# The second token chunk's attention spread over one more step of the first chunk's feed-forward loop, with a tile per block, and two weight decodings moved from steps 3 and 6 to steps 5 and 8

## The chip, the cores and the metric

The kernel runs on one core of a Trainium2 chip. The metric is the device time of one execution in microseconds (us); the time before is a median of 3 runs. Five engines with a queue each work side by side: PE (matrix products), DVE (vector work), ACT (activations and copies), POOL, and SP, which issues the transfers. Each engine executes its own queue strictly in the order in which it stands.

## What the kernel computes

```python
# windowed attention: 4 x 8 heads, 576 tokens, head size 64, each token sees the 64 up to itself
x = attn(q, k, v)                        # then heads are merged: 2304 x 512
# a dense feed-forward layer
h = x @ w_in                             # 512 -> 2048
g = where(h >= 1, h, where(h <= -1, 0, (h + 1) ** 2 / 4))
x = g @ w_out                            # 2048 -> 512
# a mixture of 8 experts, one per token
e = argmax(x @ w_gate + modality_bias[modality_id])
out = gate_w * (relu(x @ w1[e]) @ w2[e])
```

The dense weights `w_in` and `w_out` arrive as 64-bit floats and are decoded to 32 bits on the core.

## The kernel before

The 2304 tokens form 6 chunks of 384 (NC = 6); a chunk has 6 attention blocks of 64 tokens (BPC = 6), so that blocks 0 to 5 belong to chunk 0 and 6 to 11 to chunk 1. The work is software-pipelined: while chunk c goes through the feed-forward layer, the attention of chunk c+1 is done between its steps. The change touches only chunk 0's feed-forward loop, `step0(f)`, f = 0 to 15, one step for each slice of 128 hidden units. Within it the order on PE, DVE, ACT and POOL is the order in which the code is written (a manual schedule); SP's order is manual throughout.

What a step f of that loop issues, as far as the change and the prediction speak of it:

- `act2(0, f-1)` (L517, DVE): the nonlinearity of the step before, which also frees the PSUM tile `h` of that step. Tile `g` up to step 8, tile `u` after.
- `dec_clamp`, `dec_merge` (L279 to L292, DVE): eight instructions for each *pair* of weight slices that is decoded in this step. `turn[f]` lists the pairs: one for each step and a second one in the steps that `TWICE` names. `dec_abs` (L272, ACT) is the pair's first part, issued a step earlier; `dec_load` (L266, SP) fetches a pair three pairs later, once the buffer is merged.
- For the blocks of chunk 1, one new block in each of the steps 1 to 6 (`FIRST`): `att_mm` (L370, PE, scores into an `aux` PSUM tile), `att_max` (L385, DVE) and `att_exp` (L395, ACT) in the step in which a block begins; `att_norm` (L407, L408 on DVE, L416 on ACT) a step later; `att_tr` (L425, transposes on PE, copied by ACT, L430) two steps later; `att_pv` (L447, PE) and `att_x` three steps later. `att_x` copies the result into chunk 1's input, high part by ACT (`xh`, L467), low part by DVE (`xl`, L468). The `aux` tag has three PSUM buffers, used in turn by scores, transposes and results.
- `l1(0, f)` (L476, later L497, PE), `relu` (L503, L504, ACT), and `l2(0, f-2)` (L543, later L549, PE). From step FS = 9 on, the products are made of a high and a low part of each operand: `split_x0` makes them of chunk 0's input (`x0h` on ACT L349, `x0l` on DVE L350), `split_hi` and `split_lo` (L312 on ACT, L317 on DVE) of the weights.
- From step FJ = 10 on, a step also does chunk 1's first layer, `l1(1, f)`, which reads `xh` and `xl` of all six blocks 6 to 11.

Of the kernel before, what the change touches and what calls it, by code (L numbers as in the profile page):

```python
# [17 lines left out]
P = 128  # L18
# [3 lines left out]
KD = DM // P  # L22
FF = 2048
NF = FF // P
# [8 lines left out]
BPC = CT // BLK  # L33
# [38 lines left out]
def moe_kernel(ctx, tc, qT, kT, v, w_in, w_out, mod, wg, wgT, mbias, w1, w2, cst, tri, empty, out, spec):  # L72
    nc = tc.nc
    V, A, G, T, SP = nc.vector, nc.scalar, nc.gpsimd, nc.tensor, nc.sync
# [15 lines left out]
    def tile_of(shape, name, dt=F32, tag=None, bufs=1):  # L90
        pool = sb if (tag or name) in WIDE else sm
        return pool.tile(shape, dt, name=name, tag=tag or name, bufs=bufs)

    def aux(shape, name):
        return ps.tile(shape, F32, name=name, tag="aux", bufs=3)

    WB = KD * P
# [8 lines left out]
    def lend(f, lo, n=WB):  # L106
        if f not in lent:
            lent[f] = tile_of([P, 2 * WB], f"lent{f}", tag=f"T{NF + f}")
        return lent[f][:, lo * WB : lo * WB + n]
# [27 lines left out]
    def window(i):  # L137
        return (P, (i - 1) * BLK) if i % SPB else (BLK, i * BLK)

    def load_v(i):  # L140
        n, w0 = window(i) if i else (P, 0)
        if i == 1:
            vs[i] = vs[0]
            return
        vs[i] = lend(2 + i // 2, i % 2) if i < BPC else tile_of([P, DM], f"v{i}", tag="v", bufs=2)
        SP.dma_start(vs[i][:n], v[w0 : w0 + n, :])
# [57 lines left out]
    PRE = 3  # L204
    LAG = 2
    FS, FJ = 9, 10
    TWICE = (3, 6)

    def part(kind, f, lo):
        return parts[kind, f][0][:, lo * WB : (lo + 1) * WB]  # L210
# [1 line left out]
    def raw_home(p, u):  # L212
        if pairs[p][u] == lone_kf:
            return tile_of([P, WB], "lone", I32)
        if p not in raws:
            raws[p] = tile_of([P, 2 * WB], f"raw{p}", I32, tag=f"T{p}")
        return raws[p][:, u * WB : (u + 1) * WB]
# [22 lines left out]
    turn, p = [], 1  # L240
    for f in range(NF + 1):
        turn.append(list(range(p, min(p + 1 + (f in TWICE), NPR))))
        p += len(turn[-1])
# [14 lines left out]
    def words(p, u):  # L258
        w = raw(p, u).rearrange("p (n w) -> p n w", w=2)
        return w[:, :, 0], w[:, :, 1]  # L260
# [22 lines left out]
    def dec_merge(p, us=(0, 1)):  # L283
        if p < NPR:
            t = dts[p]
            for u in us:
                V.scalar_tensor_tensor(
                    t[u], words(p, u)[1], -0x40000000, t[u], op0=ALU.bitwise_and, op1=ALU.bitwise_or
                )
            for u in us:  # L290
                w = raw_home(p, u)
                V.scalar_tensor_tensor(  # L292
                    w, words(p, u)[0], 29, t[u], op0=ALU.logical_shift_right, op1=ALU.bitwise_or
                )
                whole[pairs[p][u]] = w.bitcast(F32)
# [46 lines left out]
    def split_x0(j):  # L342
        if not j:
            hi = [tile_of([P, 2 * WB], f"x0h{n}", F32R, tag=f"T{NF + 10 + n}") for n in range(2)]
            hi = [t[:, : KH * CT].rearrange("p (k n) -> p k n", k=KH) for t in hi]
            xs[0] = (hi, tile_of([P, KD, CT], "x0l", F32R, tag="xl", bufs=2))
        hi, lo = xs[0]
        ks = slice(j * KH, (j + 1) * KH)
        A.copy(hi[j], whole_x[0][:, ks])  # L349
        V.tensor_tensor(lo[:, ks], whole_x[0][:, ks], hi[j].bitcast(F32), op=ALU.subtract)  # L350

    at, xos = {}, {}
    PAIRED = 2 * BPC

    def att_sc(i):
        att_mm(i)
        att_max(i)
# [17 lines left out]
    def att_max(i):  # L375
        sc = scs.pop(i)
        n = window(i)[0]
        if i < BPC:
            s = lend(8 + i, 0).rearrange("p (k n) -> p k n", k=KD)
        else:  # L380
            s = tile_of([P, KD, P], f"s{i}", tag="s", bufs=2)
        mask = C["m1"] if i % SPB else C["m0"]
        mx = tile_of([P, KD], f"mx{i}", tag="mx", bufs=4)
        for hp in range(KD):
            V.tensor_tensor_reduce(  # L385
                s[:, hp, :n], sc[:, hp, :n], mask, -0.125, 3.0e38, ALU.add, ALU.min, mx[:, hp : hp + 1]
            )
        at[i] = (s, mx)
# [31 lines left out]
    def att_tr(i):  # L420
        s, _ = at[i]
        n = window(i)[0]
        pt = aux([P, KD, P], f"pt{i}")
        for hp in range(KD):
            T.transpose(pt[:n, hp, :], s[:, hp, :n], C["ident"])  # L425
        if i < BPC:
            ts = lend(8 + i, 1).rearrange("p (k n) -> p k n", k=KD)
        else:
            ts = tile_of([P, KD, P], f"ts{i}", tag="ts", bufs=2)
        (V.tensor_copy if i < BPC - 2 else A.copy)(ts[:n], pt[:n])  # L430
        at[i] = ts

    def att_pv(i):
        o = 0
        if i < BPC:
            xo = ps.tile([P, KD, BLK], F32, name=f"xo{i}", tag="h", bufs=2)
        elif i < PAIRED:
            xo = aux([P, KD, BLK], f"xo{i}")
        else:
            o = i % GB  # L440
            xo = xos[i - 1] if o else aux([P, KD, GT], f"xo{i}")
        ts = at.pop(i)
        vt = vs.pop(i)
        w = window(i)[0]
        for hp in range(KD):
            for a in range(2):
                T.matmul(  # L447
                    xo[a * D : (a + 1) * D, hp, o * BLK : (o + 1) * BLK],
                    vt[:w, (2 * hp + a) * D : (2 * hp + a + 1) * D],
                    ts[:w, hp, a * BLK : (a + 1) * BLK],  # L450
                    start=True,
                    stop=True,
                )
        xos[i] = xo

    def att_x(i):
        xo = xos.pop(i)
        c, n = divmod(i, BPC)
        dst = slice(n * BLK, (n + 1) * BLK)
        if i >= PAIRED:  # L460
            xos.pop(i + 1)
            dst = slice(n * BLK, n * BLK + GT)
        if c == 0:
            A.copy(whole_x[0][:, :, dst], xo)
            return
        xh, xl = xs[c]
        A.copy(xh[:, :, dst], xo)  # L467
        V.tensor_tensor(xl[:, :, dst], xo, xh[:, :, dst].bitcast(F32), op=ALU.subtract)  # L468
# [63 lines left out]
    def gsplit_lo(c, f, u):  # L532
        gh, gl = gs[c, f]
        V.tensor_tensor(gl, u, gh.bitcast(F32), op=ALU.subtract)  # L534
# [466 lines left out]
    def att_loads(i):  # L1001
        if i % GB == 0 and i + GB < NB:
            load_k(i // GB + 1)
        if i >= PAIRED:
            load_v(i)
# [42 lines left out]
    def step0(f):  # L1048
        split0 = f - 1 >= FS
        join = f >= FJ  # L1050
        at_step = {f - st: BPC + k for k, st in enumerate(FIRST)}
        if f == NF - 3:
            free.extend(f"T{NF + k}" for k in (14, 15))
        if f >= 1:
            act2(0, f - 1)
            if split0:
                gsplit_hi(0, f - 1, us[0, f - 1])
        if f - 1 >= FJ:
            act2(1, f - 1)
        for kf in soon.get(f, []):  # L1060
            split_lo()
        if split0:
            gsplit_lo(0, f - 1, us[0, f - 1])
        for p in turn[f]:
            dec_clamp(p)
            dec_merge(p)
        if 3 in at_step:
            att_pv(at_step[3])
            att_x(at_step[3])
        if 2 in at_step:  # L1070
            att_tr(at_step[2])
        if 1 in at_step:
            load_v(at_step[1])
        if 0 in at_step:
            att_mm(at_step[0])
            att_loads(at_step[0])
        for p in turn[f]:
            dec_load(p + 3)
        l1(0, f)
        relu(0, f)  # L1080
        for p in turn[f + 1][:1]:
            dec_abs(p)
        if 1 in at_step:
            att_norm(at_step[1])
        if 0 in at_step:
            att_max(at_step[0])
            att_exp(at_step[0])
        if f in (FS - 2, FS - 1):
            split_x0(f - FS + 2)
        if join:  # L1090
            l1(1, f)
            relu(1, f)
        if f >= LAG:
            l2(0, f - LAG)
        for p in turn[f + 1][1:]:
            dec_abs(p)
        for kf in soon.get(f + 1, []):
            split_hi(kf)
        if f == FS - 1:
            token_bias()  # L1100
        if f == NF - 1:
            free.extend(f"T{NF + k}" for k in (10, 11))
            hold_back(gs[0, f - 1][0].bitcast(F32))
            wgb.append(tile_of([P, E, DM], "wgb", tag="dec"))
            SP.dma_start(
                wgb[0].rearrange("p e d -> p (e d)"),
                wgT.rearrange("(o e) d -> o (e d)", o=1).broadcast_to([P, E * DM]),
            )
# [7 lines left out]
    for n in range(len(its) + LAG):  # L1116
        c, f = its[n] if n < len(its) else (NC, n - len(its))
# [151 lines left out]
```

## Time and profile before

| what | value |
| --- | --- |
| time, median of 3 runs (lowest, highest) | 736.42 us (736.12, 738.23) |
| the profiled execution: its own time, its span in the trace | 735.82 us, 734.2 us |
| PE busy | 717.1 us, 98% of the span |
| PE weight loads (PEld) busy | 625.5 us, 85% |
| DVE busy | 474.2 us, 65% |
| ACT busy | 390.1 us, 53% |
| POOL busy | 127.0 us, 17% |

Times in the rows below are counted from the start of the span. A busy time counts an engine's own instructions; the share is an average over stages that differ, and the stage that the change touches lies between 25 and 95 us of the span.

### The profile page before, as it was taken

Reading aid. Unit: us, or ns where it says so; the run is one execution under the profiler, and the core shown is the slowest. Engines: PE = TensorE matmul, PEld = TensorE weight load, DVE = VectorE, ACT = ScalarE, POOL = GpSimd, SP = SyncE. Lnnn points to the kernel's source line nnn. Section 1 sums busy time; section 2 is a strip of 40 time slices with the busy share of each in tenths; the row PEclk is TensorE's granted clock in tenths of the full one; section 3 lists DMA queues with packets and bytes.
Section 4 is the critical chain, followed back from the end, with each engine's and each line's share of the span. In section 5 each row is a group of like instructions: output and inputs, shape, how many; then the busy total and the mean of one; then the engine's idle time right before and its main releaser. Section 6 shows DMA issues by size and latency. Waiting matters only on the chain. (4 is left out here: it accounts for less than half of the span.)

```text
span 734.2 us, 12536 instructions
## 1 busy us (share of the span) xinstructions
PE 717.1 (98%) x4217; PEld 625.5 (85%) x4217; DVE 474.2 (65%) x1439; ACT 390.1 (53%) x942; POOL 127.0 (17%) x185
## 2 busy tenths in 40 slices
PE   8899999999999999999999999999999999999994
PEld 6555689888998989888989898999989989898984
DVE  5999897797397528852696638866775545453600
ACT  6777778666545535554555445645444544453511
POOL 3200000113001201120111502031058322201010
PEclk9999999999999999999999999999999999999998
DMA  9997413322121203220310015245455754444310
GB/s 327 334 346 258 147 55 127 118 66 80 52 86 59 80 15 108 73 80 16 108 59 29 2 41 171 67 93 191 158 137 171 232 181 155 159 159 160 115 43 7
DMA packets 48570, 89.26 MB, mean 122 GB/s; under 512 B 6976, under 2 KB 16320, under 8 KB 48368
## 3 DMA queue, kind: packets, MB, share of 16 engines
q1 hardware_dynamic: 44064, 78.36, 32.3%
q0 software_dynamic: 4288, 9.79, 4.6%
q8 instruction: 35, 0.57, 0.3%
q14 instruction: 39, 0.32, 0.1%
q10 hardware_dynamic: 144, 0.22, 0.1%
HBM read 78.89 MB, written 9.87 MB: 121 GB/s over the span
## 5 line engine op out<-in xcount | busy, mean ns | idle before, releaser
L497 PE MATMUL h<-xh,w 128*128 128x384 f32 x640 | 179.4, 341 | 0.0
L549 PE MATMUL py<-w,gh 128*128 128x512 f32 x522 | 162.1, 393 | 0.0
L497 PEld LDWEIGHTS h<-xh,w 128*128 128x128 f32 x640 | 117.1, 188 | 2.3
L549 PEld LDWEIGHTS py<-w,gh 128*128 128x128 f32 x522 | 96.6, 188 | 16.2
L497 PE MATMUL h<-xl,w 128*128 128x384 f32 x320 | 107.4, 336 | 0.0
L796 DVE TENSOR_TENSOR e<-wr,e 128x512 fp32r<-128x512 f32 x112 | 74.7, 690 | 45.2 <-ACT e L795 43.2
L549 PE MATMUL py<-w,gl 128*128 128x512 f32 x261 | 102.7, 396 | 0.0
L858 PE MATMUL hp<-zh,e 128*128 128x384 f32 x384 | 100.9, 336 | 0.0
L503 ACT ACTIVATE u<-h,half 128x384 f32<-128x384 f32 x96 | 55.5, 578 | 82.3 <-PE h L497 70.8
L873 PE MATMUL yo<-e,hm 128*128 128x512 f32 x348 | 99.0, 394 | 0.0
L517 DVE SCALAR_TENSOR_TENSOR u<-u,h 128x384 f32<-128x384 f32 x81 | 44.7, 552 | 68.3 <-ACT u L504 67.8
L603 DVE CUSTOM_DVE_ANT_0 prod<-y,wgb 128x512 f32<-128x512 f32 x120 | 85.3, 710 | 1.3
L529 ACT CAST gh<-u 128x384 fp32r<-128x384 f32 x81 | 41.6, 514 | 67.5 <-DVE u L517 29.1
L795 ACT CAST e<-wr 128x512 fp32r<-128x512 f32 x112 | 66.0, 616 | 18.4 <-DMA wr<-in_w 18.2
L873 PEld LDWEIGHTS yo<-e,hm 128*128 128x128 f32 x348 | 64.2, 188 | 12.4
L858 PEld LDWEIGHTS hp<-zh,e 128*128 128x128 f32 x384 | 69.6, 188 | 0.8
L418 POOL TENSOR_TENSOR s<-s,sm 128x512 f32<-128x512 f32 (+1 forms) x24 | 26.2, 1093 | 222.4 <-DVE sm L408 158.1
L858 PE MATMUL hp<-zl,e 128*128 128x384 f32 x192 | 64.3, 335 | 0.0
L534 DVE TENSOR_TENSOR gl<-u,gh 128x384 fp32r<-128x384 f32 x81 | 45.5, 562 | 26.7 <-ACT gh L529 25.7
L497 PEld LDWEIGHTS h<-xl,w 128*128 128x128 f32 x320 | 60.2, 188 | 1.9
L549 PEld LDWEIGHTS py<-w,gl 128*128 128x128 f32 x261 | 48.9, 188 | 10.4
L395 ACT ACTIVATE s<-s,mx 128x128 f32<-128x128 f32 (+1 forms) x120 | 45.9, 385 | 11.7 <-DVE mx L385 11.7
(218 smaller groups left out, 1049.5 us busy)
## 6 DMA issues: line engine op xcount, KB each, us to landing
wr<-in_w SPq DMA_DIRECT2D x112, 256.0 KB, 2.9
q<-in_qT SPq DMA_DIRECT2D x32, 256.0 KB, 3.4
dec<-in_w_in SPq DMA_DIRECT2D x16, 512.0 KB, 5.5
dec<-in_w_out SPq DMA_DIRECT2D x16, 512.0 KB, 4.3
v<-in_v SPq DMA_DIRECT2D x27, 256.0 KB, 3.0
k<-in_kT SPq DMA_DIRECT2D x15, 384.0 KB, 4.7
yd<-y SPq DMA_DIRECT2D x18, 256.0 KB, 2.2
wgb<-in_wgT SPq DMA_DIRECT2D x1, 2048.0 KB, 6.9
```

What stands on the lines that cost most here:

```text
L395: A.activation(s[:, hp, :n], s[:, hp, :n], AF.Exp, bias=mx[:, hp : hp + 1], scale=-1.0, accum_out=sm[:, hp : hp + 1],)
L497: T.matmul(h, wi(f, a)[:, k, :], b, start=n == 0, stop=n == 3 * KD - 1)
L503: A.activation(u, h, AF.Relu, bias=half, scale=0.5)
L517: V.scalar_tensor_tensor(g, u, 1.0, h, op0=ALU.min, op1=ALU.max)
L529: A.copy(gh, u)
L534: V.tensor_tensor(gl, u, gh.bitcast(F32), op=ALU.subtract)
L549: T.matmul(ys[c][t], a[:, sl], wo(f, b), start=f == first and n == 0, stop=f == last and n == 2)
L603: V.tensor_tensor_reduce(prod, yt[t], wgb[0][:, e, :], 1.0, 0.0, ALU.mult, ALU.add, lg[:, t, e : e + 1])
L795: A.copy(wpart(i, p, 0), t)
L796: V.tensor_tensor(wpart(i, p, 1), t, wpart(i, p, 0).bitcast(F32), op=ALU.subtract)
L858: T.matmul(hp, w1s(i, f, k, a), b[:, k, :], start=n == 0, stop=n == 3 * KD - 1)
L873: T.matmul(yo, a[f][:, sl], w2s(i, f, b), start=n == 0, stop=n == 3 * NF2 - 1)
```

## The change

Chunk 1's transposes move from two steps after the scores to three, its products with the values and the copies from three to four, and the loads of the values from one to two. Scores and their transposed copies get a tile for each block (`own`, on tags T18 to T23, which chunk 0's attention has used before) instead of two rotating buffers each. `TWICE` becomes steps 5 and 8, and `split_x0` moves from steps 7 and 8 to steps 6 and 7.

```diff
-    TWICE = (3, 6)
+    TWICE = (5, 8)
...
+    own = {}
...
+        elif i < PAIRED:
+            own[i] = tile_of([P, 2, WB], f"st{i}", tag=f"T{NF + 2 + i - BPC}")
+            s = own[i][:, 0].rearrange("p (k n) -> p k n", k=KD)
         else:
             s = tile_of([P, KD, P], f"s{i}", tag="s", bufs=2)
...
+        elif i < PAIRED:
+            ts = own.pop(i)[:, 1].rearrange("p (k n) -> p k n", k=KD)
         else:
             ts = tile_of([P, KD, P], f"ts{i}", tag="ts", bufs=2)
...
+        if 4 in at_step:
+            att_pv(at_step[4])
+            att_x(at_step[4])
         if 3 in at_step:
-            att_pv(at_step[3])
-            att_x(at_step[3])
+            att_tr(at_step[3])
         if 2 in at_step:
-            att_tr(at_step[2])
-        if 1 in at_step:
-            load_v(at_step[1])
+            load_v(at_step[2])
...
-        if f in (FS - 2, FS - 1):
-            split_x0(f - FS + 2)
+        if f in (FS - 3, FS - 2):
+            split_x0(f - FS + 3)
```

What the queues hold now is seen at three places. The first is DVE around the last low part of chunk 1's input: `xl` from the result `xo` of block 11, the last of six, and the nonlinearity of step 9 (`u_9`). Before:

```order
L292 SCALAR_TENSOR_TENSOR raw_995<-dec,dt_0_969 128x512
L292 SCALAR_TENSOR_TENSOR raw_995<-dec,dt_1_971 128x512
L468 TENSOR_TENSOR xl_427<-xo_998,xh_426 128x4x64
L517 SCALAR_TENSOR_TENSOR u_9_1024<-u_9_1024,h_9_1011 128x384
L317 TENSOR_TENSOR w_11_1034<-raw_874,w_11_1034 128x512
L317 TENSOR_TENSOR w_9_1036<-raw_874,w_9_1036 128x512
```

After, where `xo_975` is block 10's result and `xo_1037` block 11's:

```order
L474 TENSOR_TENSOR xl_427<-xo_975,xh_426 128x4x64
L523 SCALAR_TENSOR_TENSOR u_9_1007<-u_9_1007,h_9_994 128x384
L317 TENSOR_TENSOR w_11_1017<-raw_903,w_11_1017 128x512
L317 TENSOR_TENSOR w_9_1019<-raw_903,w_9_1019 128x512
L540 TENSOR_TENSOR gl_9_1023<-u_9_1007,gh_9_1022 128x384
L279 TENSOR_SCALAR dt_0_1010<-dt_0_1010 128x512
L279 TENSOR_SCALAR dt_1_1012<-dt_1_1012 128x512
...
L292 SCALAR_TENSOR_TENSOR raw_1034<-dec,dt_0_1010 128x512
L292 SCALAR_TENSOR_TENSOR raw_1034<-dec,dt_1_1012 128x512
L474 TENSOR_TENSOR xl_427<-xo_1037,xh_426 128x4x64
L523 SCALAR_TENSOR_TENSOR u_10_1061<-u_10_1061,h_10_1048 128x384
```

The last `xl` stood ahead of step 9's nonlinearity; it now stands behind all that step 10 issues on DVE before it: that nonlinearity, two low parts of weights, `gl` and a decoded pair.

The second place is ACT around the first high part of chunk 0's input (`x0h`). Before, in step 7:

```order
L503 ACTIVATE u_7_904<-h_7_899,half 128x384
L504 ACTIVATE u_7_904<-u_7_904 128x384
L272 ACTIVATE dt_0_907<-dec_0_828 128x512
L272 ACTIVATE dt_1_909<-dec_1_830 128x512
L416 ACTIVATE s_852<-s_852,sm_858 128x128 x4
L349 CAST x0h_917<-x_149 128x768
```

After, in step 6:

```order
L509 ACTIVATE u_6_800<-h_6_795,half 128x384
L510 ACTIVATE u_6_800<-u_6_800 128x384
L272 ACTIVATE dt_0_803<-dec 128x512
L272 ACTIVATE dt_1_805<-dec 128x512
L420 ACTIVATE st_740<-st_740,sm_746 128x128 x4
L399 ACTIVATE st_813,sm_819<-st_813,mx_814 128x128 x4
L349 CAST x0h_824<-x_149 128x768
```

The copy now also stands behind the exponentials of block 11, which the maxima of that block on DVE release; the low part `x0l` follows those maxima on DVE directly.

The third place is PE at the end of step 2 and in step 3, where `pt` is the transpose of block 6 and `sc` the scores of block 8. Before:

```order
L543 MATMUL py_2_546<-raw_434,g_0_446 128x512
L425 MATMUL pt_574<-cs,s_482 128x128 x4
L370 MATMUL sc_583<-k_462,q_464 128x128 x4
L476 MATMUL h_3_598<-x_149,raw_454 128x384 x4
L543 MATMUL py_0_544<-raw_454,g_1_493 128x512
```

After:

```order
L549 MATMUL py_2_544<-raw_434,g_0_446 128x512
L371 MATMUL sc_561<-k_462,q_464 128x128 x4
L482 MATMUL h_3_572<-x_149,raw_454 128x384 x4
L549 MATMUL py_0_542<-raw_454,g_1_493 128x512
L549 MATMUL py_1_543<-raw_454,g_1_493 128x512
L549 MATMUL py_2_544<-raw_454,g_1_493 128x512
L429 MATMUL pt_615<-cs,st_482 128x128 x4
```

The transpose of block 6 has moved behind step 3's two layers.

## Rows read from the trace of the kernel before

**Rows 1.** Windows, DVE alone: stretch and its length, busy time, granted clock, DMA
```profile
24.30:89.00 64.70, 59.91 (x172) 1.00 0.73 263
```

**Rows 2.** Waits of PE from 20 to 140 us: total, times, longest
```profile
PE pt L425 <- ACT s L416: 4.6, 3, 3.1
PE h L497 <- DVE x0l L350: 0.7, 1, 0.7
```

**Rows 3.** Waits of PE from 100 us to the end
```profile
PE rt L907 <- ACT hr L901: 0.3, 1, 0.3
```

**Rows 4.** Waits of DVE from 24.3 to 89 us
```profile
DVE x0l L350 <- ACT x0h L349: 2.8, 1, 2.8
DVE g L517 <- ACT u L504: 1.4, 2, 1.3
```

**Rows 5.** Timeline of DVE: start, duration, instruction; steps 2 to 4 begin with L517
```profile
31.83 0.56 DVE L517 SCALAR_TENSOR_TENSOR g<-u,h 128x384 f32<-128x384 f32 x1
...
36.04 0.17 DVE L407 TENSOR_SCALAR sm<-sm 128x4 f32<-128x4 f32 x1
...
37.16 0.55 DVE L517 SCALAR_TENSOR_TENSOR g<-u,h 128x384 f32<-128x384 f32 x1
...
46.23 0.55 DVE L517 SCALAR_TENSOR_TENSOR g<-u,h 128x384 f32<-128x384 f32 x1
```

**Rows 6.** Timeline of PE and ACT in step 6
```profile
61.61 1.06 PE L370 MATMUL sc<-k,q 128*128 128x128 f32 x8
...
62.50 2.75 PE L476 MATMUL h<-x,raw 128*128 128x384 f32 x8
...
65.29 0.58 ACT L503 ACTIVATE u<-h,half 128x384 f32<-128x384 f32 x1 [0.58 <-PE h L476]
```

**Rows 7.** Timeline of ACT in step 2, and in steps 6 and 7
```profile
36.46 1.28 ACT L416 ACTIVATE s<-s,sm 128x128 f32<-128x128 f32 x4 [1.24 <-DVE sm L408]
...
69.47 0.39 ACT L395 ACTIVATE s<-s,mx 128x128 f32<-128x128 f32 x1
...
71.02 0.35 ACT L467 CAST xh<-xo 128x256 fp32r<-128x256 f32 x1
...
72.57 0.58 ACT L503 ACTIVATE u<-h,half 128x384 f32<-128x384 f32 x1 [0.73 <-PE h L476]
...
74.72 1.27 ACT L416 ACTIVATE s<-s,sm 128x128 f32<-128x128 f32 x4
75.89 0.82 ACT L349 CAST x0h<-x 128x768 fp32r<-128x768 f32 x1
```

**Rows 8.** Timeline of DVE in steps 7 to 11
```profile
76.74 0.96 DVE L350 TENSOR_TENSOR x0l<-x,x0h 128x768 fp32r<-128x768 f32 x1 [2.83 <-ACT x0h L349]
77.62 0.55 DVE L517 SCALAR_TENSOR_TENSOR g<-u,h 128x384 f32<-128x384 f32 x1
...
84.17 0.55 DVE L517 SCALAR_TENSOR_TENSOR g<-u,h 128x384 f32<-128x384 f32 x1
...
88.98 0.42 DVE L468 TENSOR_TENSOR xl<-xo,xh 128x256 fp32r<-128x256 f32 x1
89.32 0.54 DVE L517 SCALAR_TENSOR_TENSOR u<-u,h 128x384 f32<-128x384 f32 x1
...
95.21 0.55 DVE L517 SCALAR_TENSOR_TENSOR u<-u,h 128x384 f32<-128x384 f32 x1
```

**Rows 9.** Timeline of PE: the first product of chunk 1 that reads `xl`
```profile
90.11 0.33 PE L497 MATMUL h<-xl,w 128*128 128x384 f32 x1
```

**Rows 10.** Groups of PE to 30 us: 128x512 products: count, busy, mean ns, idle before
```profile
L942 PE MATMUL warm<-wz 128*128 128x512 f16 x10 | 4.1, 589 | 1.3 <-DVE wz L939 1.3
L950 PE MATMUL idle<-wz 128*128 128x512 f16 x6 | 1.8, 384 | 0.0
```

**Rows 11.** Windows, PE alone, at the end of the span; columns as in the first group
```profile
725.50:728.40 2.90, 0.00 (x0) 1.00 0.04 11
728.40:734.10 5.70, 0.00 (x0) 0.51 0.02 6
```

## The prediction

> **What bounds the kernel now.** I first read who waits for PE's sake. PE is busy almost throughout, and its waits from 20 to 140 us are 4.6 us for the transposes of chunk 1's blocks (three times, 3.1 us at most) and 0.7 us for a low part of chunk 0's input [rows 2]; from 100 us to the end they are 0.3 us [rows 3]. So a delay that PE has at 97 us is still there at the end, and a gain too: PE has nothing later in which either could disappear. The change touches the stretch from 25 to 97 us, so I then read which engine is behind in it. It is DVE: 59.91 us busy of 64.70 [rows 1], with gaps of 2.8 us (for ACT's `x0h`) and 1.4 us (for ACT's `u`) [rows 4]. The transposes wait for ACT's scaling, and that waits for DVE's norm [rows 7, 5]; PE's 4.6 us are thus lateness of DVE. Last I looked for the point at which DVE's order meets PE's at the end of the stretch: the `xl` of block 11 starts at 88.98 us and lasts 0.42 us, and its first reader, the second product of `l1(1, 10)`, starts at 90.11 us [rows 8, 9]. That hand-over has 0.7 us to spare, no more.
>
> **What the change moves.** It removes no work; every instruction and transfer is issued once, as before. Three moves count.
>
> The last `xl` goes from step 9 to step 10, while its reader stays in step 10. On DVE, which is in order, step 10's nonlinearity, two low parts of weights, `gl` and a pair now stand ahead of it. In the trace these take from 89.32 to 95.21 us, 5.89 us [rows 8].
>
> A decoding pair leaves steps 3 and 6 and comes back in 5 and 8. A pair costs DVE the difference of a double and a single step: 46.23 - 37.16 = 9.07 against 37.16 - 31.83 = 5.33, so 3.74 us [rows 5]. All are done before the last `xl` either way, so the sum of DVE's work ahead of it grows by the 5.89 us alone.
>
> `split_x0` moves a step earlier. This removes PE's 0.7 us [rows 2]. But its first half now stands on ACT behind the exponentials of block 11, and DVE waits for it.
>
> DVE's gaps decide the rest, so I walk its queue with durations of the trace. Up to 37.16 us the order is the old one. Steps 3 and 4 are single: step 5 begins at 37.16 + 2 x 5.33 = 47.8. Step 5 is double, with one `xl` of 0.34 (88.98 to 89.32, [rows 8]): 9.41, so 57.2. Step 6 is single with an `xl`: DVE is through with block 11's maxima at 62.9 and wants `x0l`. PE meanwhile gets the PSUM buffer for block 11's scores when block 10's maxima have read theirs, at 57.2; the scores take 0.89 us and `relu` follows the first layer's start after 2.79 us [rows 6], so ACT begins it at 60.9. From there ACT needs 2.15 us to the scaling, 1.17 for it, 1.55 for four exponentials (69.47 to 71.02), and 0.85 from `x0h` to `x0l` [rows 7, 8]: 66.6. DVE stands still from 62.9, **3.7 us**. `x0l` takes 0.88 [rows 8]: step 7 begins at 67.5. Its norm is 4.21 us in (31.83 to 36.04, [rows 5]), plus an `xl`: 72.05. The scaling starts 0.42 us after the norm (36.04 to 36.46), then 1.17 and 0.85 to the second `x0l` [rows 5, 7, 8]: 74.5, after a gap of **2.1 us**. Step 8 begins at 75.4. It takes a step of 5.15 (84.17 to 89.32, [rows 8]) and a second pair, 8.89, and I add 0.35 because ACT has two of the new pair's parts between `x0h` and the high part of the weights that step 8 subtracts: 84.6. Step 9 takes 5.15: 89.8. With 5.89 more, the last `xl` starts at **95.7**, and its reader 0.45 later, at 96.1. Against 90.11 that is 6.0 us late [rows 9]. The totals give a second reading: 5.89 us of work and 2.0 us more of large gaps (3.7 + 2.1 + 0.35 against 4.2, [rows 4]), less the 0.7 us to spare, 7.2. The two differ because the walk has no small gaps, while the old window has 0.6 us of them (64.70 - 59.91 - 4.2, [rows 1, 4]), and by where a block has half the columns. I take **6.4**, nearer to the walk, since it follows the order. PE is there long before: the layer of chunk 0 ahead of it is free to run at about 86.
>
> What becomes of the waits of 4.6 us? The transposes now ask for a norm that is a step older, so they wait no longer; PE arrives earlier and stands at the `xl` instead. They give back nothing. The new tiles use tags that chunk 0's attention left before 22 us, and the loads of the values keep their distance to the products that free their buffers, so I cost both at nothing; the cover is a whole step, some 7 us, and without it a load would add its time at the products. On SP, what stands behind a load that waits is a score's load and two of decodings, which DVE's merges release anyway.
>
> **The clock.** From about 88 us PE has one product (with the high part) and then nothing until 96: in all some 8 us, with that one product between. In the trace PE kept its full clock through a wait of 3.1 us [rows 2, 1]; after the last products, with PE empty from 725.5 us, the granted clock went to 0.51, which is the lower level of 1.2 GHz, at about 728.4 [rows 11]. At the start of the program, where PE had done nothing, ten products took 589 ns in the mean against 384 ns for the same form later [rows 10]: 10 x 205 ns = 2.05 us for getting the clock back. No row shows the clock in the middle of the program after a gap of this kind, so the price lies between 0 and some 4 us (twice that of the start, if the clock comes back later in a longer stretch). I take **2.0 us**: the gap is nearer to the end's than to the 3.1 us.
>
> The page "TensorE: Matmul & The Clock Gate" of the Trainium skill, section "Why this matters for your kernels", tells authors to leave no long idle gaps between bursts of matmuls, since the clock goes to its lower level. By that rule the clock falls here; the sum by it is the one with the 2.0 us, without it the sum is 2.0 us less. The 3.1 us wait does not contradict it, since no row shows how much more is needed.
>
> **The sum.** 6.4 + 2.0 = 8.4 us. The profiled execution took 735.82 us, 1.6 us more than its span; with 8.4 it would take 744.2. The median is 0.6 us above it, and I give the forecast for the median: 736.42 + 8.4 = **744.8 us**.
>
> **Rivals.**
> The clock stays up: then 742.8 us. For it speaks the 3.1 us wait that cost no clock, against it that the gap is more than twice as long.
>
> DVE loses its gaps: if ACT were ahead and `x0h` ready whenever DVE asks, the 6.2 us of gaps in the walk go, the last `xl` starts at 89.5 us and its reader near 90.0. PE is then as late as before: 736.4 us, no change. Against it: both gaps follow from a chain on ACT that begins with DVE's own maxima or norm, so ACT can't be ahead.
>
> Faster: PE wins the 4.6 + 0.7 us and nothing takes their place: 731.1 us. The place is the same hand-over; it decides for a gain only if the last `xl` starts before 89.66 us on DVE (90.11 less 0.45), 6.0 us earlier than my walk has it, and for the whole gain if it starts 5.3 us before that. For it speaks that the transposes' wait is the only large one in the table. Against it stands DVE's 5.89 us of additional work. The Trainium skill's page "Perfetto Trace Analysis", section "Optimization Strategy", says a gap that repeats can mean too few buffers for the next tile. By that rule the tile per block closes the gaps, which is this rival; here the trace names ACT's scaling as the releaser, not a buffer [rows 2].
>
> Later still: one more chain on ACT, or a load of values or of a pair behind the moved doubles, costs a microsecond or two on DVE, and the clock takes twice its price: 747.6 us and more.
>
> **How the numbers follow.** Clock falls, 0.50; clock stays, 0.32; DVE without gaps, 0.07; faster, 0.05; later still, 0.06. The range is that of the first two: its lower end has the step-6 gap at its least (exponentials and copy, 1.55 + 0.85 = 2.4 instead of 3.7), no 0.35, and no clock, 6.0 - 1.65 = 4.4, so 740.8; its upper end has 4 us for the clock and the 7.2 of the totals, 11.2, so 747.6. That leaves 0.18 out. A measurement of this kernel can tell about 0.3%, 2.2 us: faster 0.05, same 0.07, slower 0.88.
>
> **What would show it.** The profile of the changed kernel should show no wait of a transpose at step 3 for ACT's scaling beyond a fraction of a microsecond; DVE waiting for `x0h` twice, near 3.7 and 2.1 us; the last `xl` near 95.7 us; PE waiting before `l1(1, 10)` for ACT's `xh` and then DVE's `xl`, some 8 us together; products of half speed, or a granted clock under 1, right behind; and no new wait of PE after 100 us. The prediction is wrong if the last `xl` starts before 92 us, if PE makes up the delay later, or if PE is held by something else in steps 3 to 9.

## The result, and the profile after

The changed kernel takes 744.87 us (median of 6 runs, 744.01 to 748.01) against 736.47 us (median of 6, 736.12 to 738.23): 8.4 us more, a ratio of 1.0117 with a 95% interval from 1.0096 to 1.0138. Its profiled execution took 744.95 us with a span of 743.2, 9.0 us longer than the span before.

DVE alone over the stretch of [rows 1], and on to the last `xl` (stretch and length, busy time, granted clock, DMA):

```profile
24.30:89.00 64.70, 58.30 (x169) 0.98 0.73 263
24.30:96.80 72.50, 66.10 (x185) 0.96 0.69 250
```

DVE has 6.4 us of gaps in the old stretch, where it had 4.8, and the stretch now goes on to 96.8 us. Its waits name them (24.3 to 96 us: total, times, longest), beside [rows 4]:

```profile
DVE x0l L350 <- ACT x0h L349: 6.0, 2, 3.9
DVE w L317 <- ACT w L312: 0.2, 1, 0.2
```

The two gaps for `x0h` are those that the walk forecast. The waits of PE from 20 to 140 us, beside [rows 2]:

```profile
PE h L503 <- DVE xl L474: 4.5, 1, 4.5
PE h L503 <- DVE g L523: 1.9, 1, 1.9
PE h L503 <- ACT xh L473: 1.8, 1, 1.8
PE sc L371 <- DMA q<-in_qT: 1.3, 1, 1.3
PE xo L453 <- ACT st L436: 1.1, 2, 0.8
PE pt L429 <- DVE xl L474: 0.6, 1, 0.6
```

The transposes' wait for ACT's scaling (`pt <- ACT s`, 4.6 us before) has gone. In its place stand 8.2 us of waits at step 10's two layers (4.5 + 1.9 + 1.8). All three are lateness of DVE: 4.5 for the `xl`, 1.9 for the nonlinearity with which step 9 begins, and 1.8 for ACT's `xh`, since ACT itself stands 3.82 us for DVE's `u` just ahead of that copy (timeline of ACT):

```profile
91.50 0.51 ACT L535 CAST gh<-u 128x384 fp32r<-128x384 f32 x1 [3.82 <-DVE u L523]
91.92 0.37 ACT L473 CAST xh<-xo 128x256 fp32r<-128x256 f32 x1
```

Smaller waits that were not there before are 1.3 us of block 8's scores for their queries, 1.1 of products with the values for ACT, and 0.6 of a transpose for DVE. From 100 us to the end PE waits for the same 0.3 us as in [rows 3]:

```profile
PE rt L913 <- ACT hr L907: 0.3, 1, 0.3
```

So nothing that PE lost before 100 us came back. The timeline of DVE (start, duration, instruction, and in brackets the idle time before it), beside [rows 5, 8]:

```profile
32.44 0.54 DVE L523 SCALAR_TENSOR_TENSOR g<-u,h 128x384 f32<-128x384 f32 x1
...
48.23 0.55 DVE L523 SCALAR_TENSOR_TENSOR g<-u,h 128x384 f32<-128x384 f32 x1
...
57.64 0.55 DVE L523 SCALAR_TENSOR_TENSOR g<-u,h 128x384 f32<-128x384 f32 x1
...
67.28 0.96 DVE L350 TENSOR_TENSOR x0l<-x,x0h 128x768 fp32r<-128x768 f32 x1 [3.90 <-ACT x0h L349]
...
75.16 0.96 DVE L350 TENSOR_TENSOR x0l<-x,x0h 128x768 fp32r<-128x768 f32 x1 [2.07 <-ACT x0h L349]
76.03 0.55 DVE L523 SCALAR_TENSOR_TENSOR g<-u,h 128x384 f32<-128x384 f32 x1
...
85.78 0.54 DVE L523 SCALAR_TENSOR_TENSOR g<-u,h 128x384 f32<-128x384 f32 x1
...
90.92 0.55 DVE L523 SCALAR_TENSOR_TENSOR u<-u,h 128x384 f32<-128x384 f32 x1
...
96.80 0.43 DVE L474 TENSOR_TENSOR xl<-xo,xh 128x256 fp32r<-128x256 f32 x1
```

Steps 5, 6, 8, 9 and 10 begin at 48.23, 57.64, 76.03, 85.78 and 90.92 us; between the last of them and the last `xl` lie 5.88 us of step 10's work. On PE the hand-over looks like this, beside [rows 9]:

```profile
86.37 0.45 PE L503 MATMUL h<-x0h,w 128*128 128x384 f32 x1 [1.86 <-DVE g L523]
...
86.98 0.97 PE L503 MATMUL h<-x0h,w 128*128 128x384 f32 x2
...
92.34 0.44 PE L503 MATMUL h<-xh,w 128*128 128x384 f32 x1 [1.83 <-ACT xh L473]
97.28 0.69 PE L503 MATMUL h<-xl,w 128*128 128x384 f32 x1 [4.50 <-DVE xl L474]
...
100.86 2.74 PE L549 MATMUL py<-lone,g 128*128 128x512 f32 x6
```

The first product that reads `xl` starts at 97.28 us, 7.17 later than before. The eleven products from there to `py` take 3.58 us (100.86 - 97.28); before, they took 1.91 (`py` at 92.02, the reader at 90.11):

```profile
92.02 2.74 PE L543 MATMUL py<-lone,g 128*128 128x512 f32 x6
```

`py` is 8.84 us late, and the span is 9.0 us longer. The granted clock shows why the products are slower (PE alone: stretch and length, busy time, granted clock, DMA):

```profile
84.00:88.00 4.00, 2.13 (x21) 0.88 0.79 285
88.00:92.00 4.00, 2.51 (x8) 0.69 0.40 132
92.00:94.00 2.00, 0.44 (x1) 0.97 1.01 416
94.00:97.00 3.00, 0.00 (x0) 0.50 0.11 45
97.00:100.00 3.00, 2.72 (x8) 0.50 0.00 0
100.00:101.00 1.00, 1.00 (x5) 0.65 0.00 0
101.00:104.00 3.00, 3.00 (x11) 1.00 0.00 0
```

PE waits for the `xl` with the clock at 0.50, the lower level of 1.2 GHz, and has the full 2.4 GHz back at about 101 us. The clock had fallen once before, behind the wait of 1.86 us: it is 1.00 from 86.4 to 87.0 us and 0.52 from 87.0 to 88.0.

### The profile page after: what moved, and what is told of

It reads as the page before. It is cut to its first block, busy times and chain, and to the rows that moved or that the text cites. A ratio compares the mean times of both kernels' runs of the same rounds, so it can differ in the third digit from the quotient of the medians.

```text
span 743.2 us, 12536 instructions
## 1 busy us (share of the span) xinstructions
PE 719.5 (97%) x4217; PEld 628.0 (84%) x4217; DVE 474.7 (64%) x1439; ACT 391.2 (53%) x942; POOL 125.2 (17%) x185
## 5 line engine op out<-in xcount | busy, mean ns | idle before, releaser
L510 ACT ACTIVATE u<-u 128x384 f32<-128x384 f32 x96 | 50.5, 526 | 2.5
```

What stands on the lines that cost most here:

```text
L510: A.activation(u, u, AF.Square)
```

## The experiments

The theory: the time is decided where the last `xl` on DVE meets its reader at the start of `l1(1, 10)`, and PE's other waits ahead of that point count for nothing. Each part of the change makes the last `xl` later, by its place in DVE's queue (the longer lag) or by gaps for ACT (the doubles, `split_x0`); the clock adds to it. The main rival: PE's own work or its waits decide, so that undoing one part gives nothing or everything back.

**One part undone, three kernels.** In the first, block 11's product with the values and its copies stand at the head of step 10 instead of behind the decoded pair.

```diff
+        if f == FJ and 4 in at_step:
+            att_pv(at_step[4])
+            att_x(at_step[4])
         if f >= 1:
             act2(0, f - 1)
...
-        if 4 in at_step:
+        if f != FJ and 4 in at_step:
```

> The changed kernel, but in step 10 the products and copies of block 11 are issued ahead of everything else of that step on PE, ACT and DVE. Theory (the last xl stands behind step 10's DVE work): that work, 5.9 us, now comes after it, so the xl starts near 90.9 us instead of 96.8 and the time falls from 744.9 to 737 to 739 us; 737.3 if the clock stays up, 739 if it still goes down. Rival (the doubled decodings in steps 5 and 8 or the earlier halves of chunk 0's input are the cause): the xl is not the point that decides, the time stays within 2 us of 744.9.

It took 738.74 us (9 runs, 736.89 to 740.64), a ratio of 1.0029 (1.0019 to 1.0039), so 6.1 us of the 8.4 went with this one move. DVE's last two `xl` stand together (timeline of DVE):

```profile
90.81 0.76 DVE L474 TENSOR_TENSOR xl<-xo,xh 128x256 fp32r<-128x256 f32 x2
```

The last of them is done 5.7 us earlier than in the changed kernel, and PE's wait for it is 0.7 us instead of 4.5. DVE's gaps for `x0h` stay at 6.0 us. The move gives the clock back too: in the trace the reader of `xl` starts at 91.62 us, 5.7 earlier, and `py` at 93.64, 7.2 earlier, since the products between run at full speed. The profiled execution took 737.38 us; why the median is 1.4 us above it is not shown.

The second and the third undo the two other parts: `TWICE` back to steps 3 and 6, and `split_x0` back to steps 7 and 8.

```diff
-    TWICE = (5, 8)
+    TWICE = (3, 6)
```

> The changed kernel with the additional decodings back in steps 3 and 6. Theory: all pairs are done before the last xl in either place, so DVE's work ahead of it is the same and only a gap of DVE shortens (3.9 to about 2.9 us): 743 to 744 us. Rival (the moved doubles are the cause): near 736.5 us.

```diff
-        if f in (FS - 3, FS - 2):
-            split_x0(f - FS + 3)
+        if f in (FS - 2, FS - 1):
+            split_x0(f - FS + 2)
```

> The changed kernel with the halves of chunk 0's input split in steps 7 and 8 as before. Theory: one of DVE's two gaps (2.1 us) goes, the other stays near 3.9 us: 742.0 to 743.0 us. Rival (the earlier split and its gaps are the whole cause): the 6 us of gaps go, about 738 us.

They took 743.79 us (4 runs; 1.0097, 1.0083 to 1.0112) and 742.5 us (5 runs; 1.0077, 1.0064 to 1.009), both as the theory had it: undoing either gives back 1 to 2.5 us. The 1.1 us of the first of them is not clear of noise (its interval overlaps that of the changed kernel, 1.0096 to 1.0138), so that here the trace has to carry the reading. DVE's waits for `x0h` from 24.3 to 96 us are, for the second kernel, two gaps of at most 2.8 us:

```profile
DVE x0l L350 <- ACT x0h L349: 4.9, 2, 2.8
```

and for the third a single one:

```profile
DVE x0l L350 <- ACT x0h L349: 3.8, 1, 3.8
```

Their last `xl` starts at 94.79 and 94.52 us, against 96.80 with all three parts, so each is some 2 us earlier. The profiled execution of the third kernel was its fastest, 740.87 us; in it the clock stayed up at the hand-over.

**One part alone, in the kernel before, three kernels.** The first has the longer lag and the tile per block (all of the change's diff but `TWICE` and `split_x0`), the second only `TWICE = (5, 8)`, the third only `split_x0` in steps 6 and 7.

> Only the later transposes and products with their own tiles; doubles in steps 3 and 6 and the split in steps 7 and 8 as before. Theory: the last xl is still in step 10, with one gap of about 2.2 us ahead of it on DVE and no wait of DVE for u: its reader is 2.5 us later than in the kernel before, plus 0 to 1.7 for the clock: 739.0 to 740.7 us. Rival (the removed 4.6 us of waits count on their own): 731.8 us.

> The kernel before with only the additional decodings in steps 5 and 8. Theory: the last xl stays in step 9, but DVE's gap for x0h grows from 2.8 to about 4.3 us and the doubles push work to where it is read: 2.1 us slower than before, 738.6 us. Rival (the moved doubles cost nothing by themselves, all pairs being done ahead of the last xl anyway): 736.5 us.

> The kernel before with only the halves of chunk 0's input split a step earlier. Theory: a second gap of about 2.1 us arises on DVE and reaches PE: 2.3 us slower than before, 738.8 us. Rival (the split a step earlier removes PE's wait of 0.7 us and no more): 735.8 us.

They took 742.48 us (5 runs; 1.0076, 1.0063 to 1.0089), 742.98 us (5 runs; 1.0087, 1.0073 to 1.01) and 739.85 us (5 runs; 1.0042, 1.0028 to 1.0055). Each part alone makes the kernel slower, so the rivals fall; but the sizes were missed, by about 2 us, 4.4 us and 1 us (the last is inside its interval). They do not add up either: 5.9, 6.4 and 3.2 us alone, 8.4 together.

The first has its last `xl` at 91.95 us and the reader at 92.43, 2.3 us late where 2.5 were forecast. The clock cost more than the 1.7 us allowed for it: the eleven products and the six of `py` behind them take 6.50 us (92.43 to 98.93), before 4.08 (90.11 to 94.19). Its profiled execution took 740.64 us, inside the forecast, and was the fastest of its five; what made the others slower is not shown.

In the two others the last `xl` is later as well (94.84 and 92.04 us), but it does not decide there: its reader on PE starts 3.2 and 2.5 us after it is done. With the doubles alone, PE is late by its waits for both parts of chunk 0's input in step 9's layer (timeline of PE):

```profile
86.64 0.44 PE L497 MATMUL h<-x0h,w 128*128 128x384 f32 x1 [1.43 <-ACT x0h L349]
90.16 0.69 PE L497 MATMUL h<-x0l,w 128*128 128x384 f32 x1 [3.07 <-DVE x0l L350]
...
98.51 0.34 PE L497 MATMUL h<-xl,w 128*128 128x384 f32 x1
```

With the early `split_x0` alone, it is late by the transposes' waits for the scaling (5.8 us in all, before 4.6) and by slow products behind the second of them, at a granted clock of 0.50:

```profile
78.36 1.35 PE L425 MATMUL pt<-cs,s 128*128 128x128 f32 x4 [2.43 <-ACT s L416]
79.51 5.33 PE L476 MATMUL h<-x,raw 128*128 128x384 f32 x8
...
94.99 0.33 PE L497 MATMUL h<-xl,w 128*128 128x384 f32 x1
```

So the theory as stated, that PE's waits ahead of the `xl` count for nothing, holds for the kernels with the longer lag so far and not for these two. What I had left out besides shows in the granted clock of PE. Of the first, the lag and the tiles alone:

```profile
34.00:44.00 10.00, 7.84 (x24) 0.83 1.05 390
84.00:94.00 10.00, 5.50 (x36) 0.83 0.30 105
```

and of the second, the doubles alone:

```profile
34.00:44.00 10.00, 6.91 (x20) 0.67 1.05 389
84.00:94.00 10.00, 5.50 (x15) 0.73 0.64 210
```

The kernel before has 1.00 in both stretches (7.09 and 9.70 us busy), with the same wait of 3.1 us for the transposes at 35 us as the kernel with the doubles alone. There the wait is followed by slow products (timeline of PE):

```profile
38.19 1.35 PE L425 MATMUL pt<-cs,s 128*128 128x128 f32 x4 [3.09 <-ACT s L416]
39.33 1.92 PE L370 MATMUL sc<-k,q 128*128 128x128 f32 x8
41.04 4.31 PE L476 MATMUL h<-x,raw 128*128 128x384 f32 x8
```

The layer of eight products takes 4.31 us instead of 2.75 [rows 6], ACT's `relu` comes later by it, and DVE, which has only one pair to decode in that step now, waits 2.70 us for that `relu` at 46.5 us. With the early `split_x0` alone the clock falls behind the same wait, but the layer takes only 2.92 us and DVE still has a second pair to decode in step 3, and its waits for `relu` stay at 1.4 us. Whether this was the cause of the miss with the doubles alone is tested next.

**The clock in the doubles alone.** Twelve products of zeros go into block 6's transposes' own PSUM tile, which the transposes then overwrite.

```diff
         pt = aux([P, KD, P], f"pt{i}")
+        for _ in range(12 if i == BPC else 0):
+            T.matmul(pt.rearrange("p k n -> p (k n)"), wz[:, :P], wz, start=True, stop=True)
```

> The kernel before with the two additional decodings in steps 5 and 8 (743.0 us, 4.4 more than forecast), and 12 products of zeros into block 6's transposes' own PSUM tile just ahead of these transposes; the transposes overwrite them. They fill some 2.6 of the 3.1 us in which PE waits for ACT's scaling; the result does not change. Theory: the 4.4 us missed there were the clock, which in the profile fell to its lower level from 37.3 to 44.1 us behind this wait, slowed step 3's products, and so made relu and DVE late as well (gaps of 4.2 us for u). With PE busy the clock stays up there, and the forecast of the queues holds: 738.6 us, up to 740.6 if the later waits for x0h and x0l still drop it once (1.003 to 1.0055). Rival: the clock is not the cause and DVE's gaps come from the moved work itself: 743.0 us as before (1.0087).

It took 740.72 us (5 runs; 1.0059, 1.0045 to 1.0073), 2.3 us less than without the products. The windows of PE:

```profile
34.00:44.00 10.00, 9.50 (x38) 1.00 1.05 392
84.00:94.00 10.00, 7.15 (x19) 0.66 0.62 213
```

The clock stays up early on, DVE's gap of 2.70 us is gone, and its last `xl` starts at 91.53 us instead of 94.84 (0.8 of these 3.3 us stood at step 2 already, 32.27 against 33.10 us, ahead of the fall), and the reader of that `xl` at 94.93 instead of 98.51; the second fall, behind waits of 1.4 and 3.1 us for `x0h` and `x0l`, stays, and with it some 2.1 us above the 738.6 of the queues alone. So the early fall was 2.3 of the 4.4 us. For the second fall its trace has a price: the five products from the `x0l` on and the six of `py` behind them take 5.40 us (86.85 to 92.25), where they took 3.16 before (84.30 to 87.46). These 2.2 us are the size of the rest, but no run undoes that fall.

The control has the same products in the kernel before:

> The control: the kernel before with the same 12 products ahead of block 6's transposes. Theory: they lie in a wait of 3.1 us and cost nothing, and the clock does not fall behind that wait in the profiled execution of the kernel before: 736.5 us (ratio 0.998 to 1.001). Rival 1: in most executions that are not profiled the clock falls there too, and the kernel before pays for it: 734 to 735.5 us (0.996 to 0.998). Rival 2: the products delay the transposes: up to 0.5 us slower.

It took 737.33 us (11 runs; 1.0011, 1.0002 to 1.0021), so the products cost 0.1 to 1.5 us (nothing in the profiled execution, whose span is 734.2 us as before) and give nothing there: no clock is to be won in the kernel before. That is just above the 1.001 of the theory and nearest to its second rival.

**The clock in the changed kernel.** Products of zeros keep PE busy at the hand-over of step 10; they go to a PSUM tile that nothing reads.

```diff
+        if f == FJ:
+            fill(4)
         l1(0, f)
...
+        if f == FJ:
+            fill(32)
         if join:
             l1(1, f)
```

> The changed kernel with 4 products of 128x512 on zeros ahead of step 10's first layer of chunk 0, and 32 ahead of that of chunk 1; their result is not used. They fill PE's gap without reaching the last xl. Theory: the clock then stays at its upper level, and the eleven products behind the xl, which took 3.6 us against 1.9 us before, take 1.9: 743.2 us, 1.7 less than the changed kernel. Rival (the slow products are slow for another reason, or the clock comes down for the waits of DVE): no change, 744.9 us.

It took 743.01 us (4 runs; 1.0094, 1.0079 to 1.011). The windows of PE:

```profile
90.00:97.00 7.00, 6.17 (x29) 1.00 0.46 150
97.00:101.00 4.00, 3.67 (x15) 1.00 0.00 0
```

The last `xl` is where it was (96.86 us), but `py` starts at 99.35 instead of 100.86. The clock is thus worth 1.5 us in the trace and 1.9 in the medians, whose intervals overlap a little; the rest of the 8.4 us is the late `xl`.

**A version that beats both.** If DVE's lateness at the hand-over is what costs the time, then it can be mended: from the changed kernel, block 11 goes to the head of step 10 as in the first experiment, `x0h` is copied on ACT in steps 4 and 5, ahead of that chain, and no step decodes a second pair.

```diff
-    TWICE = (5, 8)
+    TWICE = ()
...
+    def split_x0_hi(j):
...
+        A.copy(hi[j], whole_x[0][:, j * KH : (j + 1) * KH])
...
+        if f in (4, 5):
+            split_x0_hi(f - 4)
         l1(0, f)
```

> The changed kernel with block 11's results first in step 10, the high parts of chunk 0's input copied by ACT in steps 4 and 5 (their low parts stay in steps 6 and 7), and no doubled step at all, so that the last two pairs are decoded in steps 13 and 14. Theory: DVE has no gap ahead of the last xl and two pairs less, so no wait of PE over 0.3 us is left from step 3 on, and the 5.3 us of the kernel before and what its DVE gaps added are won: 7.0 us under the kernel before, about 729.5 us. Rival (the gain is taken back where the two pairs now stand, behind step 10): no gain over the kernel before, about 736 us.

It took 731.37 us (5 runs, 730.61 to 731.71), a ratio of 0.9926 (0.9912 to 0.994). `py` starts at 86.12 us, 5.9 earlier than before; the 7.0 expected were missed by the one wait that is left on PE from 20 to 140 us besides 0.2 us:

```profile
PE sc L374 <- DMA q<-in_qT: 1.4, 1, 1.4
```

The prediction asked only what the moved loads of the values do, and what stands behind them on SP, and put both at nothing; that this load, which does not move, meets an earlier reader is not in it. On SP it stands behind the loads of step 0's two decoded pairs; the next kernel puts it ahead of them.

```diff
-        for p in turn[f]:
+        for p in turn[f] if f > 1 else turn[0] + turn[1] if f else ():
             dec_load(p + 3)
```

> The kernel with the three steps reordered (731.4 us, 0.9926 of the kernel before), and besides the loads of step 0's two pairs of weights (512 KB each) stand on SP behind the keys and queries that step 1 fetches, instead of ahead of them. Theory: with the hand-over at xl repaired, PE's last sizeable wait is that of block 8's scores for their queries (1.4 us at 34 us); it is a queue's order and nothing else, so the queries land before 34 us, the wait goes, and the time falls by 1.0 to 1.4 us, to 730.0 to 730.4 us (0.991). Rival 1: DVE still decides at xl, so PE's gain is spent there again: 731.4 us. Rival 2: the weights that now come later are missed by DVE's merges in steps 3 and 4: 732 us or more, with DVE waiting for a transfer of dec.

It took 729.55 us (5 runs, 728.74 to 730.1), a ratio of 0.9905 (0.9884 to 0.9925), the fastest of all. All that PE waits for from 20 to 140 us is:

```profile
PE sc L374 <- DVE mx L392: 0.2, 1, 0.2
PE h L485 <- ACT x L473: 0.2, 1, 0.2
```

`py` starts at 84.93 us, 7.1 earlier than in the kernel before, and the profiled execution's span is 7.2 shorter. The 1.8 us between the two medians are more than the 1.0 to 1.4 expected, and their intervals overlap; in the traces `py` gains 1.2 us. The kernel without this last edit had gained 5.9 us at `py` and 4.2 in the span. Of the other 1.7 us some 1.1 go between 540 and 591 us, and a wait of PE of 0.3 us for `hm` stands at 502 us; the cause is open.

The last kernel asks whether the longer lag is needed at all: the kernel before, with its own lag and tiles, and only the early copies and no second pair.

```diff
-    TWICE = (3, 6)
+    TWICE = ()
...
+        if f in (4, 5):
+            split_x0_hi(f - 4)
```

> The kernel before, with its own lag of three steps and its own tiles, in which only x0h is copied earlier (on ACT in steps 4 and 5) and no step decodes a second pair. Theory: DVE decides at xl; without the two pairs ahead of it (3.74 us each) and without the 2.8 us gap for x0h, xl of block 11 comes early, and what is left is PE's own lateness: the transposes' waits of some 3 us, which need the longer lag to go. So part of the gain of the reordered kernel: 733.0 to 734.0 us (0.995 to 0.9965), against 731.4 with the lag. Rival 1: the lag brings nothing here either, and this kernel is as fast as the reordered one: 731.4 us. Rival 2: the lag brings all of it: 736.5 us.

It took 734.48 us (12 runs, 732.7 to 735.95), a ratio of 0.997 (0.9957 to 0.9983), 0.5 us more than expected. Its last `xl` starts at 84.29 us, and then it is PE that is late, by the wait that the longer lag takes away:

```profile
PE pt L428 <- ACT s L419: 3.1, 1, 3.1
```

So of the 5.2 us that the reordered kernel gains on before, 2.0 need no lag, and the other 3 or so, about the size of that wait, come with the lag, its tiles and block 11 at the head of step 10.

## Why the prediction was right, step by step

**The hand-over.** Right in place and mechanism. The last `xl` was forecast at 95.7 us and its reader at 96.1; they came at 96.80 and 97.28, so that the delay was 7.17 us for the 6.4 taken. Two terms of the walk account for it. DVE was 0.6 us late from the start of the stretch (32.44 against 31.83 us at step 2), which no moved instruction explains: 0.36 of it stood at 20 us already, ahead of all that the change touches. Step 2 begins at 32.27 to 33.10 us in the six kernels with `TWICE = (5, 8)` and at 31.76 to 32.07 in the eight others; why is open. Steps 5 to 7 then stayed 0.4 to 0.7 us behind the walk. And step 8 was mis-sized: I used step 9's 5.15 us for it, while step 8 itself took 6.55 us with 0.88 of `x0l` in it [rows 8], so 5.67. With the second pair of 3.74 and the wait of 0.2 for `w` that makes 9.61; it took 9.75 (76.03 to 85.78) for the 9.24 that I had. The reading by totals was the nearer one: 7.2 forecast, 7.17 measured, as 7.82 us at the `xl` (96.80 - 88.98) less the 0.65 that PE had to spare.

**The wait ahead of it.** That PE would stand 1.9 us at the start of step 10 for DVE's nonlinearity was not in the walk. The layer of chunk 0 began at 86.37 us all the same, where about 86 was forecast, and the `xl` came long after it. By the letter of the prediction's last sign it was held by something else in steps 3 to 9 as well (1.3, 1.1 and 0.6 us); these waits are small and were over before the hand-over.

**The gaps for `x0h`.** Forecast 3.7 and 2.1 us, measured 3.90 and 2.07, as the walk through ACT's queue had them. The 0.35 us added for ACT in step 8 were 0.2.

**Step 10's work ahead of `xl`.** 5.89 us forecast, 5.88 measured, and the first experiment gave 6.1 us of time back by this one move, the clock at the hand-over with it. It is the largest term.

**The removed waits.** Right: 4.6 us of transposes' waits for the scaling went, and PE gave the time back at the hand-over. The reordered kernels show the other half: where DVE is not late, the longer lag, with its tiles and block 11's new place, is worth some 3 us (734.48 against 731.37).

**Loads at nothing.** Right for the moved loads: PE has no wait for values in the changed kernel. But the question was too narrow, without harm to the sum: block 8's queries were 1.26 us late for PE, because PE no longer stood at the transposes ahead of those scores. I had asked whether the moved loads keep their distance, and not whether a load that is not moved is met by an earlier reader. In the changed kernel DVE decides, so it cost nothing; in the reordered one it was worth 1.2 us at `py` in the traces and 1.8 in the medians.

**The clock.** It fell, as I chose to forecast. The price of 2.0 us was 1.67 in the trace (3.58 less 1.91 us) and 1.9 in the medians of the kernel kept busy. It fell twice, which I had not foreseen; the first fall, at about 87 us, lies in front of products that end before PE's next wait, for `xh`, and so cost nothing: in the kernel kept busy, where it is absent, the last `xl` comes no earlier (96.86 us). "TensorE: Matmul & The Clock Gate" of the Trainium skill, section "Why this matters for your kernels", warns of long idle gaps between bursts of matmuls. The trace agrees for the gap of 4.50 us (0.50 behind it); for 3.1 us the runs disagree among themselves, with 1.00 behind it in the kernel before and slow products, 4.31 us for 2.75, in the doubles alone.

**The sum.** 6.4 + 2.0 = 8.4 us was met by the medians. In the profiled executions it was 7.17 + 1.67 = 8.84, so that the two errors of size, 0.8 too little and 0.3 too much, partly cancel. That the medians gave 8.4 to the tenth is luck: their interval, 1.0096 to 1.0138, is 7.1 to 10.2 us.

**The rivals.** DVE had its gaps, so "no change" fell; "faster" did not come either, but a gain of the size of its 731.1 us is there once the hand-over is mended: 731.37 and 729.55 us. Those kernels also make copies and two pairs change places, so that this is no test of the rival itself. The page that lays repeated gaps to too few buffers, "Perfetto Trace Analysis" of the Trainium skill, section "Optimization Strategy", would have had the tile per block close them. Lag and tiles were not run apart; together they closed PE's waits for the scaling, and the time still rose to 742.48 us, so the trace's naming of ACT and the order of the queues was the better guide to the time.

## What to carry to other kernels

When an instruction moves a step later in an in-order queue, add up all that now stands ahead of it on its engine, and compare it with the time that its reader has to spare: here 5.9 us of work against 0.7. A large wait of the busiest engine is worth nothing while another engine is late at the next point where the two meet, so mend that point first; the edit that cost time here is worth some 3 us once it is mended. Look for that point anew in each version of a kernel: with only the doubles moved it lay a step earlier, at chunk 0's own low part. And when a wait goes, look for what the engine now reaches earlier than its data, transfers that nobody moved among them.

## What the runs showed of the hardware

The length of a wait alone does not tell whether the clock falls. Behind the same wait of PE of 3.09 us it stayed at 1.00 in the kernel before and in the last kernel, and fell in the kernels with the doubles alone and with the early `split_x0` alone; with the doubles alone eight products then took 4.31 us instead of 2.75; and in the changed kernel it fell at about 87 us behind a wait of only 1.86 us, with 0.32 us and a few small products ahead of it. What tells these apart was not settled. A fall early in a stretch can be passed on: slow products make ACT and then DVE late, with the doubles alone by a gap of 2.70 us. Twelve products of zeros in the wait bought back 2.3 us where the clock fell, and bought nothing where it did not.
